# Three numbers of a planner: first products, second keys and token sums of a gated mix of attention and MLP

## The chip, the cores and the metric

The kernel runs on one core of one Trainium2 chip. The metric is the device time of one execution in microseconds (us), the median of several runs. Engines are named as in the profile: PE is TensorE's matmul (PEld its weight load), DVE is VectorE, ACT is ScalarE, POOL is GpSimd, SP is SyncE, whose queue issues the DMAs. L553 is line 553 of the kernel.

## The reference, cut to what matters

The input is x of 2048 tokens by 448. Two branches read it, and a gate per token mixes them. Everything is float32.

```
g = sigmoid((x * gate_w).sum(-1))
# branch A: 16 heads of 28, each token sees 8 keys: itself and 2, 4, ... 14 tokens back
q, k, v = split(x @ wqkv)
logits  = einsum(q, k at those 8 positions) * 28 ** -0.5   # -1e9 before the first token
a = (softmax(logits) weighted sum of v at those positions) @ wo
# branch B: hidden size 1792
h = relu(x @ w1 + b1) ** 2
b = h @ w2 + b2
out = g * a + (1 - g) * b
```

## The kernel before, in words

**Precision.** A float32 matmul is made of three products of float32r parts: high by high, high by low, low by high. So each operand is split: ScalarE writes the high part (a copy), VectorE subtracts it and writes the low part. `split_full` does that from SBUF. `split_copied` (L726) first has ScalarE copy the raw tile into one PSUM bank, the copy bank, and lets VectorE read from there (L738); the bank is single, so the next copy (L733) waits for the low part of the one before.

**Stages.** The 2048 tokens are reordered into four chunks of 512, two of each parity, so that a token's keys all lie in its own parity. Phase A computes q, k and v of chunks 0, 1, 2 and 3 in this order. Chunk 0 is `qkv_first`. Chunks 1 and 3 are two calls of `qkv_two` each, one for two token tiles. Chunk 2 is `qkv_seven`, which forms the 2 by 2 block product with seven products, and for that needs sums of tokens, made by `token_sums(2)` (six steps, 900 apart in the plan: four on VectorE, L962 and L963, then two that split the sums, `s_1` and `s_0`). Each result is evacuated from PSUM by ScalarE (`qkv_evacuate`, L234; `copied`, L428) or added to a stage by VectorE (`added`, L432) and stored to DRAM (`stage_store`, L226) as q_d, k_d, v_d. Within `run`, a VectorE write (`turn`, L211) into an accumulator lets its two row groups change places.

Phase B runs the MLP chunk by chunk, in the order 3, 0, 1, 2: hidden layer (`h_first`, `h_second`), square and split of it (`mlp_ops`, L852 to L855), second layer (`o_part`). Its first two hidden pairs (`mlp_one`, `mlp_two`) are put into the last call of `qkv_two`. Here w1 and w2 are split too (`w1_piece`, `w2_piece`), timed to end before they are read.

**Attention** runs beside all of this. It has eight units: two parities by four groups of four heads. For a unit, `att_load_qk` loads q and k from DRAM (L524, L525) into tiles that have one buffer each. Eight products `qk_piece` on GpSimd (L553) are each reduced by VectorE (L554); a softmax in three steps follows, then eight products with v (`av_piece`, L560), reduced by L568. Products go through a pool of four buffers. `attention` interleaves the units: the qk products of unit i, then the av products of unit i - 1.

**What sets the order.** Nothing is scheduled automatically: each engine runs its instructions in the order in which Python wrote them. Two clocks steer that order. `clock["pe"]` adds the estimated time of each batch of matmuls: `advance(dt)` adds dt, first emits everything that is due (entries of `later`, set by `when` and `at` with planned times in ns), and then lets the attention generator emit as long as `clock["att"]` is behind. Each product yields its planned cost (`QK_COST`, `AV_COST`, `SM_COST`), which moves `clock["att"]`. The costs do not delay anything on the chip; they only decide beside which matmuls, and so behind which other instructions, a product, its reduction or a load is written. `piece` calls `flush(DEFER)` after each product, which emits the oldest reductions until two are left pending.

The generator starts when chunk 1 is stored (`st_["spilled"] = 0`, `clock["on"] = True`). It emits the loads of unit 0 and waits `ATT_DELAY`; then eight products of unit 0 are planned `QK_COST` apart; the loads of unit 1 come directly after the eighth (L659); then it waits `KEY_DELAY` before the first product of unit 1:

```
                if i == 1:
                    yield KEY_DELAY
                q, k = qk.pop(i)
                for s in range(NS):
                    yield piece(lambda: qk_piece(i, q, k, lgs[i], s), QK_COST)
...
                    if i == 0:
                        qk[1] = att_load_qk(*units[1])
```

Other planned times that stand near: `when(82000.0 ...)` of w1's last piece, `when(85500.0, w2_piece, 0, ...)`, the load of the first four rows of w2, and `when(76300.0 ...)` for w1's third piece (L1027 to L1032).

Of the kernel before, what the change touches and what calls it, by code (L numbers as in the profile page):

```python
# [30 lines left out]
MM512 = 227.0  # L31
MM448 = 203.0
QK_COST = 2300.0
AV_COST = 2000.0
SM_COST = 600.0
ATT_DELAY = 17000.0
# [7 lines left out]
LOAD_DELAY = 1500.0  # L44
LAND_DELAY = 5000.0
OL_DELAY = 2500.0
KEY_DELAY = 6000.0
DEFER = 2
ORDER = (3, 0, 1, 2)
WARM = 13  # L50
# [6 lines left out]
def gated_mix_kernel(ctx: ExitStack, tc: tile.TileContext, xT, wqkv, w1, w2, wo, b1, b2, out):  # L57
# [306 lines left out]
    class Group:  # L364
# [12 lines left out]
        def token_sums(self, n, j):  # L377
            a, b = sums[self.c, (None, 1, 0, 0, 1)[n]], (None, 1, 0, 1, 0)[n]
            o = (2 * self.u + b) * P if j < 2 else CH + b * P
            return tuple(t[:, o:o + P] for t in a)  # L380
# [140 lines left out]
    def att_load_qk(par, g):  # L521
        q = attp.tile([P, NS, C], F32, tag="q", name=f"q{par}{g}")
        k = kv_tile("k", f"k{par}{g}")
        nc.sync.dma_start(q, q_d[par, g].rearrange("(p s) c -> p s c", s=NS))  # L524
        nc.sync.dma_start(k, halo_ap(k_d, par, g))  # L525
        return q, k

    def att_load_v(par, g, tag="v"):
        v = kv_tile(tag, f"v{par}{g}")
        nc.sync.dma_start(v, halo_ap(v_d, par, g))  # L530
        return v
# [10 lines left out]
    def flush(n):  # L542

        m = 2
        while len(pending) > n and m:
            if quiet[0] and pending[0] in exps_due:
                return
            pending.pop(0)()
            m -= 1

    def qk_piece(u, q, k, lg, s):
        pr = prodp.tile([P, W, C], F32, tag="pp", name=f"qk{u}_{s}", bufs=PP_BUFS)
        nc.gpsimd.tensor_mul(pr, q[:, s:s + 1].to_broadcast([P, W, C]), k[:, s:s + W])  # L553
        pending.append(lambda: nc.vector.tensor_reduce(  # L554
            lg[:, s], pr.rearrange("p w (h d) -> p w h d", h=HG), axis=AX.X, op=ALU.add))

    def av_piece(u, par, g, v, lg, s):

        pr = prodp.tile([P, C, W], F32, tag="pp", name=f"av{u}_{s}", bufs=PP_BUFS)
        nc.gpsimd.tensor_mul(  # L560
            pr.rearrange("p (h d) w -> p w h d", h=HG),
            lg[:, s][:, :, :, None].to_broadcast([P, W, HG, DH]),
            v[:, s:s + W].rearrange("p w (h d) -> p w h d", h=HG),
        )
        o = o_t[par, s]

        def rest():
            nc.vector.tensor_reduce(o[:, g * C:(g + 1) * C], pr, axis=AX.X, op=ALU.add)  # L568

            def out():  # L570
                nc.vector.transpose(o, o)
                at(OUT_DELAY, lambda: o_store(par, s))
            if g == G - 1 and par:
                out()
            elif g == G - 1:

                at(s * OUT_GAP, out)
        pending.append(rest)
# [5 lines left out]
    def softmax(u, lg):  # L584

        lgv = lg.rearrange("p s w h -> p s h w")
        mx = smp.tile([P, NS, HG], F32, tag="mx", name=f"mx{u}")
        sm = smp.tile([P, NS, HG], F32, tag="sm", name=f"sm{u}")

        def masked():  # L590
            nc.gpsimd.tensor_add(lg, lg, mask[:, :, :, None].to_broadcast([P, NS, W, HG]))
            pending.append(lambda: nc.vector.tensor_reduce(mx, lgv, axis=AX.X, op=ALU.max))

        def exps():
            nc.gpsimd.tensor_sub(lg, lg, mx[:, :, None].to_broadcast([P, NS, W, HG]))

            def rest():
                nc.scalar.activation(lg, lg, AF.Exp, scale=SCALE)

            def sums():  # L600
                nc.vector.tensor_reduce(sm, lgv, axis=AX.X, op=ALU.add)
                nc.vector.reciprocal(sm, sm)
            exps_due.append(rest)
            pending.extend([rest, sums])

        def norm():
            nc.gpsimd.tensor_mul(lg, lg, sm[:, :, None].to_broadcast([P, NS, W, HG]))

        return [masked, exps, norm]
# [9 lines left out]
    def attention():  # L619


        lgs, vs, qk = {}, {}, {}
        n = len(units)
        soft = []

        loads = []

        def piece(fn, cost):
            fn()
            flush(DEFER)  # L630
            while loads and not hold[0]:
                loads.pop(0)()
            return cost

        def soft_step():
            return piece(soft.pop(0), SM_COST)

        for i in range(n + 1):
            if i < n:
                par, g = units[i]  # L640
                while st_["spilled"] < par:
                    yield None
                if i not in qk:
                    qk[i] = att_load_qk(par, g)
                if i == 0:
                    vs[0] = att_load_v(par, g)
                    yield ATT_DELAY
                lgs[i] = smp.tile([P, NS, W, HG], F32, tag="lg", name=f"lg{i}")
                if i == 1:
                    yield KEY_DELAY  # L650
                q, k = qk.pop(i)
                for s in range(NS):
                    yield piece(lambda: qk_piece(i, q, k, lgs[i], s), QK_COST)

                    if soft and (s == 2 or (i == 1 and s in (4, 7))):
                        yield soft_step()
                if i + 1 < n and units[i + 1][0] <= st_["spilled"]:
                    if i == 0:
                        qk[1] = att_load_qk(*units[1])  # L659
                    else:  # L660
                        loads.append(lambda i=i: qk.update({i + 1: att_load_qk(*units[i + 1])}))
                soft.extend(softmax(i, lgs[i]))
            if i >= 1:
                par, g = units[i - 1]
                v, lg = vs.pop(i - 1), lgs.pop(i - 1)
                for s in range(NS):
                    if g == 0:
                        assert len(o_t) < NS
                        o_t[par, s] = opool.tile([P, D], F32, tag="o", name=f"o{par}_{s}", bufs=NS)
                    yield piece(lambda: av_piece(i - 1, par, g, v, lg, s), AV_COST)  # L670
                    if soft and (s in (2, 5) or (i == n - 1 and s == 7)):
                        yield soft_step()
                    if i == n - 1 and s == 1:

                        loads.append(lambda i=i: vs.update({i: att_load_v(*units[i], "k")}))
                if i < n - 1:
                    loads.append(lambda i=i: vs.update({i: att_load_v(*units[i])}))
                if g == G - 1:
                    while pending:
                        flush(0)  # L680
                    st_["att"] = par

    att = attention()
    clock = {"pe": 0.0, "att": 0.0, "on": False}
    later = []
# [227 lines left out]
    def when(t, fn, *args):  # L913
        later.append((t, lambda: fn(*args)))
# [61 lines left out]
    def steps(t, gap, fns):  # L976
        for i, fn in enumerate(fns):
            when(t + i * gap, fn)
# [41 lines left out]
            when(t + 5000.0, lambda c: x_spill(c, xs[c]), c)  # L1020
    when(23500.0, x_more, 2)
    when(39500.0, x_more, 3)
    when(46000.0, lambda: steps(46100.0, 900.0, token_sums(2)))
    when(10500.0, x_spill, 0, x)
    when(25000.0, w1_piece, 0, 38000.0, 2000.0)
    when(44500.0, halos)
# [326 lines left out]
    for g in range(2, 2 * NF):  # L1353
        i, f = g // (NF // 2), g % (NF // 2) * 2
# [121 lines left out]
```

## Time and profile before

| | us |
|---|---|
| median of 3 runs | 417.91 (417.07 to 418.85) |
| the profiled execution's own time | 416.63 |
| its span, first to last instruction | 414.8 |
| TensorE busy | 407.4 |
| GpSimd busy | 267.1 |
| VectorE busy | 279.1 |
| ScalarE busy | 219.8 |

The granted TensorE clock is 1.0 in all slices. The times of rows are microseconds from the span's start. A row of the timeline has the start, the time from the first start to the last end of what it merges, the engine, the line, the operation, output and input with their shapes, and the count; in brackets stands how long the engine was idle before it, and the engine and line that ended the wait. A row of DMA issues ends with the median time from the issue to the landing.

### The profile page before, as it was taken

Reading aid. Unit: us, or ns where it says so; the run is one execution under the profiler, and the core shown is the slowest. Engines: PE = TensorE matmul, PEld = TensorE weight load, DVE = VectorE, ACT = ScalarE, POOL = GpSimd, SP = SyncE. Lnnn points to the kernel's source line nnn. Section 1 sums busy time; section 2 is a strip of 40 time slices with the busy share of each in tenths; the row PEclk is TensorE's granted clock in tenths of the full one; section 3 lists DMA queues with packets and bytes.
Section 4 is the critical chain, followed back from the end, with each engine's and each line's share of the span. In section 5 each row is a group of like instructions: output and inputs, shape, how many; then the busy total and the mean of one; then the engine's idle time right before and its main releaser. Section 6 shows DMA issues by size and latency. Waiting matters only on the chain.

```text
span 414.8 us, 9364 instructions
## 1 busy us (share of the span) xinstructions
PE 407.4 (98%) x3817; PEld 363.9 (88%) x3817; DVE 279.1 (67%) x454; ACT 219.8 (53%) x498; POOL 267.1 (64%) x167
## 2 busy tenths in 40 slices
PE   8999999999799999999999999999999999999997
PEld 8999999989688888888888888989898888888996
DVE  4674874576586867777755897979676677792344
ACT  4674786398475566444565535444643254346640
POOL 0000000960999999989999999899989978950000
PEclk9999999999999999999999999999999999999999
DMA  7999899968263415554020569965146530058304
GB/s 212 344 380 350 237 379 288 373 204 268 92 234 159 158 50 179 204 187 152 2 83 2 175 230 271 259 149 154 36 151 210 205 129 0 31 159 156 103 2 179
DMA packets 66492, 74.00 MB, mean 178 GB/s; under 512 B 32464, under 2 KB 58768, under 8 KB 66320
## 3 DMA queue, kind: packets, MB, share of 16 engines
q1 hardware_dynamic: 66448, 73.39, 55.3%
q8 instruction: 30, 0.49, 0.5%
q14 instruction: 14, 0.11, 0.1%
HBM read 45.94 MB, written 28.25 MB: 179 GB/s over the span
## 4 chain that ended last, share of the span: by engine, by line
PE 89%; DVE 3%; ACT 3%; DMA 2%; POOL 2%; issue 1%; SPq 0%; DVEq 0%; POOLq 0%
PE b L201 32%; PE h L201 30%; PE qkv L201 11%; PE a L201 7%; PE qkv L282 2%; DMA k<-k_d 2%; PE v L335 2%; POOL qk L553 2%; PE x L335 1%; DVE lg L554 1%; PE warm L865 1%; PE a L1248 1%; ACT x L997 1%; PE z L335 1%; DVE st L432 1%
## 5 line engine op out<-in xcount | busy, mean ns | idle before, releaser
L553 POOL TENSOR_TENSOR qk<-q,k 128x896 f32<-128x896 f32 x64 | 134.4, 2129 | 92.3 <-DMA k<-k_d 71.2
L560 POOL TENSOR_TENSOR av<-lg,v 128x896 f32<-128x896 f32 x64 | 118.7, 1954 | 3.3 <-DVE lg L554 2.8
L852 DVE TENSOR_TENSOR h<-h,h 128x512 fp32r<-128x512 f32 x56 | 38.5, 688 | 59.9 <-ACT h L855 59.5
L554 DVE TENSOR_REDUCE lg<-qk 128x32 f32<-128x896 f32 x64 | 67.2, 1075 | 4.8 <-POOL qk L553 4.7
L568 DVE TENSOR_REDUCE o<-av 128x112 f32<-128x896 f32 x64 | 66.7, 1070 | 1.4 <-POOL av L560 1.4
L201 PE MATMUL b<-w2bh,h 64*128 64x448 f32 x448 | 66.2, 360 | 0.4 <-DVE h L852 0.4
L201 PE MATMUL b<-w2ah,h 64*128 64x448 f32 x448 | 66.3, 359 | 0.0
L853 ACT ACTIVATE h<-h,b1z 128x512 f32<-128x512 f32 x56 | 36.7, 656 | 42.1 <-PE h L201 42.1
L201 PE MATMUL qkv<-wqh,x 64*128 64x448 f32 (+1 forms) x384 | 57.7, 361 | 0.6 <-DVE qkv L211 0.6
L201 PEld LDWEIGHTS b<-w2bh,h 64*128 64x128 f32 x448 | 42.0, 184 | 4.3 <-DVE h L852 0.7
L201 PEld LDWEIGHTS b<-w2ah,h 64*128 64x128 f32 x448 | 41.9, 184 | 3.7
L201 PE MATMUL b<-w2bl,h 64*128 64x448 f32 x224 | 40.6, 358 | 0.0
L201 PE MATMUL b<-w2al,h 64*128 64x448 f32 x224 | 40.5, 358 | 0.0
L201 PEld LDWEIGHTS qkv<-wqh,x 64*128 64x128 f32 x384 | 36.6, 184 | 3.7 <-DVE qkv L211 1.1
L201 PE MATMUL qkv<-wql,x 64*128 64x448 f32 (+1 forms) x192 | 35.3, 360 | 0.0
L854 ACT ACTIVATE h<-h 128x512 fp32r<-128x512 f32 x56 | 33.5, 599 | 1.7
L855 ACT ACTIVATE h<-h 128x512 f32<-128x512 f32 x56 | 33.2, 593 | 0.0
L800 ACT ACTIVATE h<-h 128x4 fp32r<-128x4 f32 (+1 forms) x35 | 7.2, 207 | 43.8 <-PE b L201 43.7
L234 ACT ACTIVATE st<-qkv 128x448 f32<-128x448 f32 x36 | 18.2, 542 | 15.8 <-PE qkv L201 9.0
L201 PEld LDWEIGHTS b<-w2bl,h 64*128 64x128 f32 x224 | 21.1, 184 | 1.9
L201 PEld LDWEIGHTS b<-w2al,h 64*128 64x128 f32 x224 | 21.0, 184 | 1.9
L201 PEld LDWEIGHTS qkv<-wql,x 64*128 64x128 f32 x192 | 18.4, 184 | 1.3
(257 smaller groups left out, 829.6 us busy)
## 6 DMA issues: line engine op xcount, KB each, us to landing
k<-k_d SPq DMA_DIRECT2D x8, 840.0 KB, 6.4
v<-v_d SPq DMA_DIRECT2D x8, 840.0 KB, 4.7
x_d<-x SPq DMA_DIRECT2D x12, 512.0 KB, 8.0
q_d<-st SPq DMA_DIRECT2D x8, 448.0 KB, 5.7
k_d<-st SPq DMA_DIRECT2D x8, 448.0 KB, 6.1
v_d<-st SPq DMA_DIRECT2D x8, 448.0 KB, 5.3
w1raw<-w SPq DMA_DIRECT2D x4, 896.0 KB, 9.9
q<-q_d SPq DMA_DIRECT2D x8, 448.0 KB, 3.8
```

The source lines that it names most:

```text
L201: nc.tensor.matmul(acc.pt[:, :acc.n], a[rows], w[rows], start=acc.todo == acc.all, stop=acc.todo == 1)
L234: nc.scalar.activation(st[:, :, t % 2], heads(pt), AF.Copy)
L282: nc.tensor.matmul(acc.pt[:, :D], a, w, start=k == j == 0, stop=False)
L335: nc.tensor.matmul(self.pt[:, :self.n], a, w, start=new, stop=True, skip_group_check=True)
L553: nc.gpsimd.tensor_mul(pr, q[:, s:s + 1].to_broadcast([P, W, C]), k[:, s:s + W])
L554: pending.append(lambda: nc.vector.tensor_reduce(lg[:, s], pr.rearrange("p w (h d) -> p w h d", h=HG), axis=AX.X, op=ALU.add))
L560: nc.gpsimd.tensor_mul(pr.rearrange("p (h d) w -> p w h d", h=HG), lg[:, s][:, :, :, None].to_broadcast([P, W, HG, DH]), v[:, s:s + W].rea ...
L568: nc.vector.tensor_reduce(o[:, g * C:(g + 1) * C], pr, axis=AX.X, op=ALU.add)
L852: nc.vector.tensor_sub(hl, pt, f32(hh))
L853: ops += [lambda pt=pt, r=r: nc.scalar.activation(pt, pt, AF.Relu, bias=b1t[:, f + r:f + r + 1]), lambda pt=pt, hh=hh: nc.scalar.activatio ...
L854: lambda pt=pt, hh=hh: nc.scalar.activation(hh, pt, AF.Square),
L855: lambda pt=pt, r=r, low=low: (nc.scalar.activation(pt, pt, AF.Square), at(delays[r], low))]
```

## The change

Three numbers of the plan change. The products of unit 0 are planned 2130 apart instead of 2300; `KEY_DELAY` grows from 6000 to 7300; and the token sums of chunk 2 are planned from 44,600 on instead of 46,100. No instruction is added or removed, no tile or wait is changed by hand: what changes is the order in which instructions are written into the engines' queues.

```diff
 QK_COST = 2300.0
+QK_FIRST = 2130.0
 AV_COST = 2000.0
...
-KEY_DELAY = 6000.0
+KEY_DELAY = 7300.0
...
                 for s in range(NS):
-                    yield piece(lambda: qk_piece(i, q, k, lgs[i], s), QK_COST)
+                    yield piece(lambda: qk_piece(i, q, k, lgs[i], s), QK_COST if i else QK_FIRST)
...
-    when(46000.0, lambda: steps(46100.0, 900.0, token_sums(2)))
+    when(44500.0, lambda: steps(44600.0, 900.0, token_sums(2)))
```

## The prediction

> **What bounds the kernel now.** I read the page first, then TensorE's waits, then the chain of waits where they fall.
>
> ```profile
> span 414.8 us, 9364 instructions
> ...
> PE 407.4 (98%) x3817; PEld 363.9 (88%) x3817; DVE 279.1 (67%) x454; ACT 219.8 (53%) x498; POOL 267.1 (64%) x167
> ```
> ```profile
> PE h L201 <- ACT st L234: 2.1, 1, 2.1
> ...
> PE qkv L201 <- DVE qkv L211: 0.6, 1, 0.6
> ```
>
> TensorE works 407.4 of 414.8 us. No matmul is added or removed, so the time can change only through the 7.4 us in which it stands still. These two waits are single stalls, of 2.1 and 0.6 (columns: total, times, longest); they are the part that this change can reach. The chain of waits shows what feeds the larger (columns: start, length, what):
>
> ```profile
> 93.90 0.36 SPq L226
> ...
> 94.35 0.46 SPq L226
> ...
> 94.91 0.84 SPq L524
> ...
> 95.80 7.20 DMA k<-k_d
> ...
> 103.16 6.31 POOL qk L553 x3
> ...
> 109.49 1.09 DVE lg L554
> 110.58 0.54 DVE w2al L738
> ...
> 111.14 0.55 ACT copy L733
> 111.69 0.47 ACT st L234
> ...
> 112.20 2.99 PE h L201 x23
> ```
>
> The second unit's keys are asked for at 95.80, behind two stores (93.90, 94.35) that wait for ScalarE. They land at 103.0. GpSimd's third product ends at 109.47; its reduction holds VectorE's queue, behind it stand a low part (L738), ScalarE's copy, and the evacuation (L234) that frees the accumulator for the next hidden layer. TensorE starts at 112.20, and the timeline has the wait to two digits:
>
> ```profile
> 112.20 0.50 PE L201 MATMUL h<-x,w17h 64*128 64x512 f32 x1 [2.14 <-ACT st L234]
> ```
>
> so it had been idle since 110.06. GpSimd, meanwhile, stood still from 89.30 to 103.16:
>
> ```profile
> 72.58 16.72 POOL L553 TENSOR_TENSOR qk<-q,k 128x896 f32<-128x896 f32 x8 [71.19 <-DMA k<-k_d]
> 103.16 6.30 POOL L553 TENSOR_TENSOR qk<-q,k 128x896 f32<-128x896 f32 x3 [13.85 <-DVE w2al L738]
> ```
>
> The second row names a VectorE instruction as releaser. This is it:
>
> ```profile
> 102.40 0.63 DVE L738 TENSOR_TENSOR w2al<-copy,w2ah 128x448 fp32r<-128x448 f32 x1 [0.61 <-ACT copy L733]
> ```
>
> It ends at 103.03, within a few hundredths of the load; a product reads neither of its tiles, so I take the load, as the chain does.
>
> **The change, part by part.**
>
> *The keys' request (QK_FIRST and KEY_DELAY).* The planner's clock stands at 51,156 when attention is switched on, so the first product is planned at 68,155. Eight products of 2300 put the second unit's loads at 86,555; eight of 2130 put them at 85,195. The planning step that covers 85,195 ends at 85,260, the stores are written after the one that ends at 85,869. So both loads now stand ahead of the two stores, and also ahead of the w2 load that was planned for 85,500. They can't run at once: q and k have one buffer each, and the first unit reads them until 72.58 + 16.72 = 89.30. SyncE waits there, then issues q at about 89.3 and k at 89.7. Where they land comes from these rows (size, median us from issue to landing, first of the whole run, then of 86 to 100 us):
>
> ```profile
> k<-k_d SPq DMA_DIRECT2D x8, 840.0 KB, 6.4
> ...
> w1raw<-w SPq DMA_DIRECT2D x4, 896.0 KB, 9.9
> q<-q_d SPq DMA_DIRECT2D x8, 448.0 KB, 3.8
> ```
> ```profile
> w2raw<-w SPq DMA_DIRECT2D x1, 896.0 KB, 5.2
> k<-k_d SPq DMA_DIRECT2D x1, 840.0 KB, 7.2
> ...
> q_d<-st SPq DMA_DIRECT2D x1, 448.0 KB, 2.8
> ```
>
> 448 KB land in 3.8 and 896 KB in 5.2, so 448 KB more cost 1.4. q lands at 93.1, k 2.6 later at 95.7; by k's own medians 96.1 to 96.9. GpSimd starts some 7 us sooner and has three products by 96 + 6.3 = 102.3. The three reductions then follow VectorE's earlier work without waiting: below that work ends 1.04 later than before, at 103.03 + 1.04 = 104.1; three reductions of 1.05 end at 107.2, L738 (0.54), the copy (0.55) and L234 (0.47) at 108.8. TensorE wants the accumulator at 110.06 + 1.04 = 111.1. **The stall of 2.14 goes**, with 2.3 us to spare; k could land as late as 102 before any of it returned. Bounds: -2.14 to 0, I take -2.14.
>
> *What the shorter first products do to VectorE.* Planning unit 0 tighter moves its products to earlier planning steps, and each emission flushes an older reduction into VectorE's queue. The third product moves from the step ending at 73,080 to 72,471, the fourth from 77,343 to 74,907, the fifth (77,355 to 76,675) from 79,779 to 77,343, the eighth from 85,260 to 83,433; the others keep their step. So reduction 0 now precedes the additions of z, reduction 1 those of x, and **reduction 2 moves ahead of the first w1 low part** (L738, planned for 77,600). Before, that queue read:
>
> ```profile
> 78.03 1.15 DVE L432 TENSOR_TENSOR st<-z,st 128x448 f32<-128x448 f32 x2
> 79.09 1.08 DVE L554 TENSOR_REDUCE lg<-qk 128x32 f32<-128x896 f32 x1
> 80.09 1.15 DVE L432 TENSOR_TENSOR st<-x,st 128x448 f32<-128x448 f32 x2
> ...
> 82.14 0.61 DVE L738 TENSOR_TENSOR w1bl<-copy,w1bh 128x448 fp32r<-128x448 f32 x1
> ...
> 88.44 1.08 DVE L554 TENSOR_REDUCE lg<-qk 128x32 f32<-128x896 f32 x1
> ```
> ```profile
> 82.79 0.55 ACT L733 ACTIVATE copy<-w1raw 128x448 f32<-128x448 f32 x1 [0.85 <-DVE w1bl L738]
> ```
> ```profile
> 89.65 0.47 PE L201 MATMUL qkv<-wqh,x 64*128 64x448 f32 x2 [0.57 <-DVE qkv L211]
> ```
>
> GpSimd has product 2 by 72.58 + 3 x 2.09 = 78.9, so nothing waits for it. One reduction (79.09 to 80.09 is 1.00; with its tail 1.08) then stands before the low part, which starts at 83.2 instead of 82.14. ScalarE's copy waited for just that low part; it uses the one copy bank, and copies, low parts and x copies alternate from there without a gap to the fifth reduction at 88.44 and the L211 write behind it, for which TensorE waited 0.57 at 89.08. Reduction 2 used to run later, in a gap that this chain leaves to VectorE while ScalarE works; now it is on the chain. I move the chain by **1.04**: TensorE restarts at 90.7 and the 0.57 becomes 1.6. Bounds: 0 (a gap that I do not see swallows it) and +2.0 (reduction 0 also counts). The swaps of reductions 0 and 1 with additions of the same queue free TensorE's accumulators 1.0 later: z's first at 79.65 for a matmul that began at 79.85. That is a margin of 0.2; without it the cost is under 0.3.
>
> *The w2 load that now stands behind.* It was issued at 93.1 - 5.2 = 87.9 and now comes at 90.2. By the 1.4 per 448 KB it lands 2.8 after k, at 98.5. ScalarE reads it first at:
>
> ```profile
> 96.96 0.60 ACT L732 ACTIVATE w2ah<-w2raw 128x448 fp32r<-128x448 f32 x1
> ...
> 102.64 0.98 ACT L234 ACTIVATE st<-qkv 128x448 f32<-128x448 f32 x2 [0.28 <-PE qkv L201]
> ```
> ```profile
> 103.64 0.40 PE L201 MATMUL h<-x,w17h 64*128 64x512 f32 x2
> ```
>
> that is 98.0 with the shift. It is 0.5 late. Cover: ScalarE idles 0.28 before L234, whose first half (0.49) ends 0.5 before the hidden-layer matmul at 103.64, so 0.75 of lateness is free. I take 0; a load that takes 9.9, like w1raw of the same size, lands at 100.1 and costs 2.1 - 0.75 = 1.35, and 2.25 if both issues ahead take the 0.84 of q's in the chain, so that it starts 0.9 later. The rows show the order this rests on: store, store, q and k, issued at 93.90 to 95.80, land last with k. [...]
>
> *Token sums 1.5 sooner.* Their six ScalarE parts now stand before the evacuation of chunk 1's last q and k:
>
> ```profile
> 54.44 0.98 ACT L234 ACTIVATE st<-qkv 128x448 f32<-128x448 f32 x2 [0.74 <-PE qkv L201]
> 55.45 1.38 ACT L129 ACTIVATE s_1h<-xraw 128x512 fp32r<-128x512 f32 x3
> 56.85 1.38 ACT L129 ACTIVATE s_0h<-xraw 128x512 fp32r<-128x512 f32 x3
> ```
> ```profile
> q_d<-st SPq DMA_DIRECT2D x1, 448.0 KB, 8.9
> ```
>
> They take 2 x 1.38, ScalarE was idle for 0.74 ahead of the evacuation, so this and its stores come some 2.0 later. Attention's first load waits for them, but here the store took 8.9 to land (row of 50 to 60 us) against 2.8 from an idle queue: 6.1 of backlog hides it. I take 0; bounds 0 and, the cover gone, 2.0 on attention's start; sooner sums gain nothing, since TensorE waits for nothing between its start and the 0.57 below 90 us.
>
> *Later products* come 60 ns earlier in the plan (1360 - 1300). By the planner's arithmetic thirteen cross a planning step, and two of their reductions overtake a hidden layer's low part, these:
>
> ```profile
> 132.39 0.69 DVE L852 TENSOR_TENSOR h<-h,h 128x512 fp32r<-128x512 f32 x1 [1.42 <-ACT h L855]
> ```
> ```profile
> 210.56 0.69 DVE L852 TENSOR_TENSOR h<-h,h 128x512 fp32r<-128x512 f32 x1 [1.00 <-ACT h L855]
> ```
>
> VectorE idles 1.42 and 1.00 ahead of them, room for one reduction each: 0, at most 0.1.
>
> **Sum**: -2.14 + 1.04 + 0 + 0 + 0 = -1.1. The profiled execution took 416.63 (414.8 and 1.83 around it), so 415.5 for it; the median of the runs is 417.91, 1.28 above, and I predict 417.91 - 1.1 = **416.8**.
>
> **The rivals.**
> *A. Both effects are gains.* VectorE absorbs reduction 2 and the 0.57 stays or goes: 417.9 - 2.14 to - 2.7 = 415.2 to 415.8. For it: VectorE is two thirds busy. Against: the copy at 82.79 waited for L738.
> *B. The w2 load takes the stall's place.* Landing after 98.75 it makes ScalarE late, and the hidden layer at 104.7 waits. From 99.85 on the change loses: with 1.35, 418.2; with 2.25, 417.9 - 1.1 + 2.25 = 419.1. For it: 1288 KB ahead in the queue. Against: that queue was empty when q is issued.
> *C. Token sums delay attention by 2.0* (the backlog is less than it looks): keys at 97.7 still suffice, but w2raw lands at 100.5, 2.5 late, 1.75 of stall: 417.9 - 2.14 + 1.04 + 1.75 = 418.6. For it: the evacuation does come later. Against: the 6.1.
>
> **How the numbers follow.** Forecast 0.55 (416.2 to 417.4), A 0.2, B 0.17, C 0.08. What a measurement can tell is 0.5%, 2.09 us: faster means under 415.8, slower over 420.0. A lies almost wholly under the first, and a little of the forecast: 0.2. B and C reach the second only if both meet or the load is later still: 0.07. Same 0.73. Range 415.1 (A's faster end and its 0.1) to 418.8 (C, and most of B).
>
> **What would show it.** k's request at about 89.7, ahead of the two stores; GpSimd idle 7 us, not 13.85; no wait for L234 near 110. TensorE's wait for L211 near 89 at 1.6, the decisive row between forecast and A. ScalarE's first L732 on w2 at about 98.5, waiting for its load; a TensorE wait near 104.7 would be B. A first product later than 72.6 would be C. Wrong altogether if the 2.1 is still there with keys in by 97, or if the hidden layers' low parts show new waits after 120.

## The result and the profile after

The kernel after takes 415.47 us (median of 20 executions, 415.0 to 417.99), the kernel before 418.02 (20 executions, 416.74 to 418.85): a ratio of 0.995, 95% interval 0.9937 to 0.9963. That is 2.55 us or 0.6%, with an interval on both sides of the 0.5% that the prediction takes as the least that can be told, and 1.3 below the predicted 416.8. It lies inside the range of 415.1 to 418.8, but below the forecast's own 416.2 to 417.4 and within the 415.2 to 415.8 of rival A, which expected two gains. The profile shows that it is not A. One execution in all that follows, of the kernel with one added product, took 509.54 us at a mean clock of 0.755 and is left out of its counts.

The page of after, its head and its first part:

```profile
span 415.0 us, 9362 instructions
...
PE 407.5 (98%) x3817; PEld 389.4 (94%) x3817; DVE 278.5 (67%) x454; ACT 220.2 (53%) x498; POOL 268.1 (65%) x167
```

The profiled execution took 416.86 us, 0.23 more than the one of before, in spite of the gain. Here are TensorE's waits in it (us in total, times, longest); all lines after 34 stand one higher than before:

```profile
PE qkv L202 <- DVE qkv L212: 1.6, 1, 1.6
...
PE h L202 <- ACT st L235: 0.8, 1, 0.8
PE qkv L283 <- DVE x L896: 0.5, 1, 0.5
```

The wait of 2.1 for L234 (L235 in after) is gone. The 0.6 has become 1.6, as forecast. There is a new 0.8, which is not the old one: it lies near 106, in the hidden layer ahead of it. The 0.5 is the start's, behind the first load of x; no part of the change reaches it, and the profile of before has none.

The timeline of after has the keys' request ahead of everything, and the load of w2 behind it:

```profile
90.19 0.33 SPq L525 DMA_DIRECT2D q<-q_d  x1
90.57 0.42 SPq L526 DMA_DIRECT2D k<-k_d  x1
91.09 0.38 SPq L779 DMA_DIRECT2D w2raw<-w  x1
```
```profile
95.95 6.31 POOL L554 TENSOR_TENSOR qk<-q,k 128x896 f32<-128x896 f32 x3 [5.79 <-DMA k<-k_d]
```

GpSimd idles 5.79 instead of 13.85 and has its third product at 102.26, not 109.47. On VectorE, reduction 2 stands ahead of the first low part (L739, before L738), and TensorE's wait follows:

```profile
82.73 1.07 DVE L555 TENSOR_REDUCE lg<-qk 128x32 f32<-128x896 f32 x1
83.72 0.61 DVE L739 TENSOR_TENSOR w1bl<-copy,w1bh 128x448 fp32r<-128x448 f32 x1
```
```profile
91.22 0.47 PE L202 MATMUL qkv<-wqh,x 64*128 64x448 f32 x2 [1.55 <-DVE qkv L212]
```

The chain of waits of after (start, length, what) shows where the 0.8 comes from:

```profile
91.09 9.73 DMA w2raw<-w
...
105.83 0.53 ACT st L235
...
106.41 2.79 PE h L202 x18
```

The load of w2 took 9.73 us, not the 5.2 of before. It landed at 100.82; ScalarE's first high part of w2 waited for it, and ScalarE with its alternation of high parts and copies was late for the evacuation that TensorE needed:

```profile
100.84 0.58 ACT L733 ACTIVATE w2ah<-w2raw 128x448 fp32r<-128x448 f32 x1 [2.16 <-DMA w2raw<-w]
```
```profile
106.41 0.50 PE L202 MATMUL h<-x,w17h 64*128 64x512 f32 x1 [0.76 <-ACT st L235]
```

That is the mechanism of rival B, in this execution.

**Where the time went, by stage.** TensorE's order is the same in both kernels, so four of its instructions serve as milestones: the last product of y, the first of the hidden layer that starts near 104, the first of the second layer near 118, the last of all. The rows of before (the one at 103.64 stands in the prediction):

```profile
65.64 0.36 PE L335 MATMUL y<-wqh,x 64*128 64x448 f32 x2
...
118.41 0.36 PE L201 MATMUL b<-w2ah,h 64*128 64x448 f32 x2
...
411.40 0.27 PE L1248 MATMUL last<-woh,o 128*128 128x224 f32 x1
```

and of after:

```profile
66.23 0.36 PE L336 MATMUL y<-wqh,x 64*128 64x448 f32 x2
...
105.26 0.39 PE L202 MATMUL h<-x,w17h 64*128 64x512 f32 x1
...
118.32 0.36 PE L202 MATMUL b<-w2ah,h 64*128 64x448 f32 x1
...
411.63 0.27 PE L1249 MATMUL last<-woh,o 128*128 128x224 f32 x1
```

From y to the hidden layer: 38.00 us before, 39.03 after, +1.03. From there to the second layer: 14.77 before, 13.06 after, -1.71. The rest: 292.99 and 293.31. So the two forecast effects are both there. Yet 14.77 - 13.06 holds a gain and the late load in one number, and neither it nor the forecast -1.1 explains 2.55 between the medians. The experiments take these apart.

### The profile page after: what moved, and what is told of

It is laid out like the page before. It is cut to its first block, busy times and chain, and to the rows that moved or that the text cites. A ratio compares the mean times of both kernels' runs of the same rounds, so it can differ in the third digit from the quotient of the medians.

```text
span 415.0 us, 9362 instructions
## 1 busy us (share of the span) xinstructions
PE 407.5 (98%) x3817; PEld 389.4 (94%) x3817; DVE 278.5 (67%) x454; ACT 220.2 (53%) x498; POOL 268.1 (65%) x167
## 4 chain that ended last, share of the span: by engine, by line
PE 89%; DVE 3%; DMA 3%; ACT 2%; issue 1%; SPq 0%; DVEq 0%
PE b L202 32%; PE h L202 32%; PE qkv L202 11%; PE a L202 7%; DMA w2raw<-w 2%; PE qkv L283 2%; PE v L336 2%; PE x L336 1%; DVE lg L555 1%; ACT copy L734 1%; DMA xraw<-xT 1%; PE a L1249 1%; PE z L336 1%; DVE st L433 1%; PE y L336 1%
## 5 line engine op out<-in xcount | busy, mean ns | idle before, releaser
L202 PE MATMUL b<-w2ah,h 64*128 64x448 f32 x448 | 74.3, 359 | 0.0
L202 PE MATMUL b<-w2bh,h 64*128 64x448 f32 x448 | 72.9, 360 | 0.4 <-DVE h L853 0.4
L202 PEld LDWEIGHTS b<-w2ah,h 64*128 64x128 f32 x448 | 57.5, 184 | 0.4
L202 PEld LDWEIGHTS b<-w2bh,h 64*128 64x128 f32 x448 | 54.5, 184 | 1.7 <-DVE h L853 0.7
L202 PE MATMUL b<-w2al,h 64*128 64x448 f32 x224 | 53.8, 358 | 0.0
L202 PE MATMUL b<-w2bl,h 64*128 64x448 f32 x224 | 51.4, 359 | 0.0
L202 PEld LDWEIGHTS b<-w2al,h 64*128 64x128 f32 x224 | 33.1, 184 | 0.1
L202 PEld LDWEIGHTS b<-w2bl,h 64*128 64x128 f32 x224 | 31.0, 184 | 0.4
L235 ACT ACTIVATE st<-qkv 128x448 f32<-128x448 f32 x36 | 17.9, 542 | 15.2 <-PE qkv L202 12.3
```

The source lines that it names most:

```text
L202: nc.tensor.matmul(acc.pt[:, :acc.n], a[rows], w[rows], start=acc.todo == acc.all, stop=acc.todo == 1)
L235: nc.scalar.activation(st[:, :, t % 2], heads(pt), AF.Copy)
```

## The experiments

The same milestones were read for each profile, in the same way; the table gathers the start of the last product of y and the three differences, in us. "Clock" is the mean granted TensorE clock of that execution.

| kernel | y at | y to hidden layer | hidden layer to second layer | rest | clock |
|---|---|---|---|---|---|
| before | 65.64 | 38.00 | 14.77 | 292.99 | 1.0 |
| before, again | 67.99 | 37.98 | 16.09 | 293.19 | 0.996 |
| after | 66.23 | 39.03 | 13.06 | 293.31 | 1.0 |
| after, again | 65.37 | 38.99 | 12.05 | 292.98 | 1.0 |
| keys alone | 67.97 | 37.98 | 13.37 | 293.26 | 1.0 |
| products alone | 66.04 | 39.04 | 14.79 | 293.04 | 1.0 |
| token sums alone | 65.94 | 37.98 | 16.14 | 293.33 | 0.996 |
| after, w2 first | 65.73 | 39.17 | 12.05 | 293.01 | 0.999 |
| keys alone, w2 first | 65.96 | 38.02 | 12.05 | 293.01 | 1.0 |
| before, seven added products | 65.64 | 37.96 | 14.82 | 293.15 | 1.0 |

The first column differs by up to 2.6 us between executions, with the change and without it, and the 1.74 between after and the keys alone arise in the first 15 us: in the keys alone products still start 0.37 us apart beyond 8 us, in after 0.20 apart from about 6.4 us on, with a mean granted clock of 1.0 in both executions. Two products in a row show it by their length, 0.95 and 0.56:

```profile
8.12 0.95 PE L282 MATMUL qkv<-wql,x 128*128 128x448 f32 x2
```
```profile
7.15 0.56 PE L283 MATMUL qkv<-wql,x 128*128 128x448 f32 x2
```

Why they start farther apart is not settled. So the profiled executions' own times (417.74 for the keys alone, with a median of 415.62) can't be compared; the stages and the medians can.

### The change in parts

**The whole change again.** No edit.

> The changed kernel once more, beside its parts. Theory 1 (the forecast's steps): -1.1 to -2.2 us against the kernel before; TensorE's waits are about 1.55 at L212 near 91 us, none for L235 near 110, and 0 to 0.8 for L235 near 106, as late as the w2 load lands. Theory 2 (the reduction moved ahead costs nothing, everything comes from the keys): the wait at L212 is back at 0.6 in an execution whose first matmul does not wait. Theory 3 (the size is set by how fast loads land in an execution): the span and the wait near 106 move together with the landing time of the w2 load, between 5 and 10 us.

415.63 us, ratio 0.9941 [0.9918, 0.9964]. TensorE's wait for L212 was 1.6 again, which rules out theory 2. In this profile the load of w2 was issued at 89.86 and took 7.5 us by the view of DMA issues, and ScalarE, busy until its first high part of w2, did not wait for it:

```profile
w2raw<-w SPq DMA_DIRECT2D x1, 896.0 KB, 7.5
```
```profile
97.64 0.60 ACT L733 ACTIVATE w2ah<-w2raw 128x448 fp32r<-128x448 f32 x1
```

TensorE had no wait near 106, and the stage took 12.05. So the late load costs 1.0 (13.06 - 12.05) in one execution and nothing in another of the same kernel.

**The keys alone.** The eighth product's planned cost is lowered instead of all eight, so that the loads come early and no reduction moves; the token sums stay.

```diff
-                    yield piece(lambda: qk_piece(i, q, k, lgs[i], s), QK_COST)
+                    yield piece(lambda: qk_piece(i, q, k, lgs[i], s), QK_COST if i or s < NS - 1 else QK_COST - 1360.0)
...
-KEY_DELAY = 6000.0
+KEY_DELAY = 7300.0
```

> Only the request of the second unit's keys moves ahead of the stores and the w2 load; the eighth product's planned cost is cut by 1360 instead of 170 per product, so that VectorE's order around the first unit stays that of before; token sums as before. Theory 1: wait near 89 stays 0.57, wait near 110 goes (-2.14), but ScalarE is 1.0 earlier at the w2 rows than in the changed kernel, so a w2 load that lands at 98.5 to 100.8 costs 0.8 to 3.1 near 104; in all -1.3 to +1, and not better than the changed kernel by more than 0.5. Theory 2: -2.1, the same as the changed kernel.

415.62 us, ratio 0.9949 [0.9927, 0.9972]: as good as the whole. That is 2.6 below the median of before beside it (418.23), more than theory 1's -1.3 to +1 allows; below is why. From y to the hidden layer it has before's 37.98, so the price of the shorter products is not paid. But its w2 load, behind the keys as in after, was late in the profile:

```profile
101.84 0.58 ACT L732 ACTIVATE w2ah<-w2raw 128x448 fp32r<-128x448 f32 x1 [2.46 <-DMA w2raw<-w]
```

and the next stage took 13.37 instead of 12.05. ScalarE, without the 1.04 of delay, reaches this load sooner, which fits the larger price (1.32 here, 1.01 in after): what the keys alone save at one place they pay in part at the other.

**The shorter products alone.** The first seven products are planned 2130 apart, the eighth makes up the difference, so that the loads stay where they were.

```diff
-                    yield piece(lambda: qk_piece(i, q, k, lgs[i], s), QK_COST)
+                    yield piece(lambda: qk_piece(i, q, k, lgs[i], s), QK_COST if i else 2130.0 if s < NS - 1 else 3490.0)
...
-KEY_DELAY = 6000.0
+KEY_DELAY = 5940.0
```

> Only the products of the first unit are planned 2130 apart; the loads of the second unit keep their place in SyncE's queue (the eighth product's planned cost takes up the rest), token sums as before. Theory 1: the wait at L211 near 89 grows from 0.57 to 1.55, the wait near 110 stays but is filled from the other side: the evacuation is 1.0 later as well, so the whole is +0.5 to +1.1. Theory 2: 0, the wait near 89 stays at 0.6.

419.57 us, ratio 1.0035 [1.0012, 1.0058]: slower, by an interval that leaves out no change, and 1.3 above the median of before beside it, a little more than the expected +0.5 to +1.1. Its timeline has the forecast wait, 1.53 against 0.57 before, and the old stall unchanged behind it:

```profile
91.03 0.47 PE L201 MATMUL qkv<-wqh,x 64*128 64x448 f32 x2 [1.53 <-DVE qkv L211]
```
```profile
113.68 0.50 PE L201 MATMUL h<-x,w17h 64*128 64x512 f32 x1 [2.17 <-ACT st L234]
```

**The token sums alone.**

```diff
-    when(46000.0, lambda: steps(46100.0, 900.0, token_sums(2)))
+    when(44500.0, lambda: steps(44600.0, 900.0, token_sums(2)))
```

> Only the token sums are planned 1500 sooner. Theory 1: 0 (-0.3 to +0.3): the evacuation of chunk 1's last q and k ends 2.0 later, the stores wait in a full queue anyway, and attention's first product starts at 72 to 73 us as before. Rival (the sums matter): a first product later or sooner by over 0.5 us, or a change of over 0.5 us in the time.

418.41 us, ratio 1.0004 [0.9982, 1.0026]: nothing. GpSimd's first product starts at 72.65, as expected. Its profile has waits of 2.2 and 0.6, as before; and yet its stage from the hidden layer to the second layer took 16.14 us, 1.37 more than in the profile of before. The end of its stall and the windows of that stretch (window, its length, busy time and count of PE, PEld, DVE, ACT, POOL, then the granted clock of TensorE, the DMA share and GB/s) show why:

```profile
112.55 0.50 PE L201 MATMUL h<-x,w17h 64*128 64x512 f32 x1 [2.21 <-ACT st L234]
```
```profile
110.00:112.00 2.00, 0.34 (x3) 0.00 (x0) 1.45 (x2) 0.51 (x2) 2.00 (x2) 1.00 0.00 0
112.00:114.00 2.00, 1.45 (x12) 1.22 (x14) 1.29 (x3) 2.00 (x6) 2.00 (x2) 0.99 0.28 95
114.00:116.00 2.00, 2.00 (x12) 1.53 (x12) 2.00 (x3) 1.97 (x4) 2.00 (x3) 0.50 1.02 332
116.00:118.00 2.00, 2.00 (x16) 1.86 (x14) 1.96 (x4) 1.52 (x5) 2.00 (x2) 0.65 0.10 33
118.00:120.00 2.00, 2.00 (x20) 1.73 (x19) 1.69 (x2) 1.20 (x5) 2.00 (x2) 1.00 0.00 0
```

Some 1.4 us behind the end of the stall (112.55; by the 0.99 the fall lies near 113.96), TensorE's granted clock falls to a half, and then is full again. Work lost: 2 x (0.01 + 0.50 + 0.35) = 1.72 us, which at half clock is 3.4 us of time. In before's profile it was 1.00 in all of these windows. From its first hidden-layer product to its last of all this kernel took 309.47, before 307.76: 1.71 more. TensorE's busy time shows it too, 409.2 against 407.4 with the same number of instructions, while the time in which it stood still hardly differs (7.6 and 7.4):

```profile
PE 409.2 (98%) x3817; PEld 397.2 (95%) x3817; DVE 279.2 (67%) x454; ACT 220.1 (53%) x498; POOL 267.6 (64%) x167
```

### The clock behind the stall

This gave a second theory of the gain: the stall near 110 has a price beyond its length, because in some executions the clock drops behind it. The results give the mean clock of every execution timed for the experiments; here those at 0.995 or 0.996 are called low and the others full. Over 116 executions of before, 56 had 0.995 or 0.996, with a median of 418.75 us, and 60 had 0.999 or 1.0, with 416.98: 1.77 apart, the 1.72 of the windows. Kernels without the stall (after, after again, the keys alone: 44 executions) were at 0.998 or above in every one; with the stall kept, 9 of 12 (products alone) and 7 of 12 (token sums alone) were low. Full with full and low with low, the products alone are 1.2 and 1.1 us above the executions of before beside them, close to the forecast price of 1.04 (3 and 9 executions); the token sums alone are 0.2 and 0.1 above. Six runs test it.

**Before, again.** No edit.

> The kernel before against itself: ratio 0.998 to 1.002. Theory 'clock': about half of its executions have a mean granted clock of 0.995 to 0.996 and take some 1.7 us longer than those at 0.999 to 1.0; where the profiled execution is one of them, the clock is at about half speed from some 1.5 us behind the end of the idle stretch near 110 for about 3.3 us, and nowhere else. Theory 'waits only': the two groups have the same time, or the low clock lies elsewhere.

417.79 us, ratio 0.9995 [0.9971, 1.0018]. 5 of 12 executions were low (median 418.84) and 7 full (416.81). The profiled one was low, and its windows have the same picture in the same place, behind a stall of 2.14; to its last product it took 309.28 from the first of the hidden layer, 1.52 more than in before's profile:

```profile
114.54 0.50 PE L201 MATMUL h<-x,w17h 64*128 64x512 f32 x1 [2.14 <-ACT st L234]
```
```profile
114.00:116.00 2.00, 1.46 (x12) 1.19 (x14) 1.30 (x3) 2.00 (x6) 2.00 (x2) 0.92 0.29 96
116.00:118.00 2.00, 2.00 (x12) 1.56 (x10) 2.00 (x3) 1.97 (x4) 2.00 (x3) 0.50 1.02 332
118.00:120.00 2.00, 2.00 (x18) 1.80 (x16) 1.95 (x4) 1.31 (x5) 2.00 (x2) 0.73 0.10 31
```

**Work put into the stall.** Seven products ahead of the block that stalls, into the bank that is free; the wait for the other bank ends when it did.

```diff
-    def h_first(x, c, f):
+    def h_first(x, c, f, fill=0):
...
         accs = [Acc("m", f"h{c}_{f + r}", CH) for r in range(2)]
+        for _ in range(fill):
+            nc.tensor.matmul(accs[0].pt[:, :CH], w17h[0:64, f // 2 * P:f // 2 * P + P], x.x7[0:64], start=True, stop=True)
...
-        pair[1] = h_first(xm[3], ORDER[0], 2)
+        pair[1] = h_first(xm[3], ORDER[0], 2, fill=7)
```

> The kernel before with seven more products of 64 x 512 put on TensorE just before the first real product of the block that stalls near 110 (same operands as that product, into its own bank, which the real product then starts anew); every other engine has the same instructions in the same order. Each takes about 0.23 us by the rows near 109, so they fill 1.6 us of the 2.14 us for which TensorE stands idle near 110, and the product that waits for the bank freed at 112 starts when it did. Theory 'clock' (the idle stretch near 110 halves TensorE's granted clock for about 3.3 us behind it in about half of the executions, as in the profile of the token sums alone, where 1.7 us were lost between 114 and 118): the mean granted clock is 0.998 to 1.0 in every execution instead of 0.995 to 0.996 in about half of them, and the median falls by 0.7 to 1.7 us, ratio 0.996 to 0.9985. Theory 'waits only' (the split of the granted clock has to do with the execution, not with the stall): no change, ratio 0.999 to 1.001, and half of the executions at 0.995 to 0.996. Both: the wait for the bank near 112 ends when it did.

416.92 us, ratio 0.9968 [0.9948, 0.9987], and 0 of 12 executions low. The waits of TensorE fall to

```profile
PE h L201 <- ACT st L234: 0.6, 1, 0.6
```

while the stage takes 14.82, as in before: no time was saved at full clock (416.92 against 417.08 for the full-clock executions of before beside it), and the median still fell by 1.5. Before beside it had 14 of 23 low. It is the clock that was saved. This kernel does only useless work more, and is faster.

**Less work in the stall.** One such product, then three, and three again on another chip.

> The kernel before with one more product of 64 x 512 ahead of the block that stalls near 110 (seven left 0.6 us of the 2.1 us of waiting and no execution with a lowered clock). It leaves about 1.9 us. Theory 'clock by length': the share of executions with a lowered granted clock falls from about half to something between none and half, and each such execution still loses about 1.8 us; the median lies between 416.9 and 418.7 accordingly. Rival 'a threshold between 1.6 and 2.1 us that this passes': the share stays at about half, or is none.

> The same with three more products, which leave about 1.45 us. The kernel after waits 1.55 us near 91 and no execution of it had a lowered clock, so by either theory none is expected here: all executions at 0.998 to 1.0 and a median of 416.8 to 417.1. If some are lowered, the length of the wait alone does not decide it.

> The three half products again, on the same chip as the whole ones. Both theories: 4 to 6 of 12 executions with a lowered clock, those about 1.8 us longer than the others. None, or all, would say that the share differs too much from chip to chip to be compared.

Ratios 0.9993 [0.9971, 1.0015], 1.0001 [0.9979, 1.0023] and 1.0003 [0.998, 1.0025]. Low executions: 3 of 11, 5 of 12 and 4 of 12 (before beside them 9 of 23 and 9 of 23). With so few executions, 3 of 11 can't be told from 9 of 23. The expectation for three products was wrong: the profiled waits were 1.2 (a full execution) and 1.6 us (a low one), like the 1.55 of after near 91 or shorter, and none of after's executions was low. So the length of the wait alone does not decide it.

**Three products over the whole array.** The same three, over 128 rows of the array instead of 64.

```diff
-            nc.tensor.matmul(accs[0].pt[:, :CH], w17h[0:64, f // 2 * P:f // 2 * P + P], x.x7[0:64], start=True, stop=True)
+            nc.tensor.matmul(accs[0].pt[:, :CH], w17h[:, f // 2 * P:f // 2 * P + P], x.x7, start=True, stop=True)
```

> The three added products ahead of the block near 110, now over all 128 rows of the array instead of 64 (same time each, bank and place). With three of 64 rows the wait was 1.2 us and 5 of 12 executions had a lowered clock, although the kernel after waits 1.55 us near 91 and had none in 32. Theory 'work in the window': what lowers the clock is how little the array did over some microseconds, and products over half of its rows count half; counted so, the kernel before loses 2.5 us of work there, three half products leave 2.2, seven (no lowered execution) 1.7, and three whole ones 1.8: no or few lowered executions, at most 2 of 12, median 416.8 to 417.2. Theory 'time in the window': whole products count as half ones, 4 to 6 of 12 lowered, median 416.8 to 418.5. In both the wait is 1.2 us and the time of the executions at full clock 416.3 to 417.5.

417.34 us, ratio 0.9996 [0.9976, 1.0017]; 0 of 12 low, against 9 of 24 with the half products. But the wait was not the expected 1.2. The waits of the whole products and, below, of the half ones on the same chip:

```profile
PE h L201 <- ACT st L234: 0.9, 1, 0.9
```
```profile
PE h L201 <- ACT st L234: 1.6, 1, 1.6
```

So this fits the theory that work is what counts, but work and length of the wait were both changed, and it does not separate them. The median shows no gain here: its executions, all full, were 0.3 above the full ones of before (417.34 against 417.02), and at 417.32 the median of before lay just on the full side of its two groups (14 full, 9 low).

### The late load, and a better kernel

**After, with w2 first.** The load is due 0.5 us sooner in the plan, and so is written ahead of the second unit's q and k.

```diff
-    when(85500.0, w2_piece, 0, 4, 92500.0, 1400.0)
+    when(85000.0, w2_piece, 0, 4, 92500.0, 1400.0)
```

> The kernel after with the w2 load due 0.5 us sooner in the plan, so that SyncE issues it ahead of the second unit's queries and keys instead of behind them. The load then lands about 2 us or more sooner and its first high part no longer waits for it; the keys are asked for 0.6 us later and land about 0.6 to 1 us later, GpSimd's first product of the second unit with them, still ahead of the VectorE work that the products feed. Theory 'w2 load late': the wait near 106 (0.76 us in one profile of after, none in the other) is gone in every execution, median 0 to 0.8 us below after's, that is 414.8 to 415.6, ratio 0.992 to 0.994. Rival 'keys late again': a part of the wait near 110 comes back, 415.6 to 417.

415.11 us over 6 executions, ratio 0.993 [0.9904, 0.9957]. w2 landed in 5.4 us and k in 7.6 (view of DMA issues), GpSimd started at 97.81, and no stall came back: the only single waits are 1.5, the known 1.2 at the start and 0.4. The stage takes 12.05.

**The keys alone, with w2 first.** The edit of the keys alone and this one together.

> The kernel before with the second unit's keys asked for early by the cost of the eighth product alone (no reduction moves ahead on VectorE, token sums where they were) and with the w2 load due 0.5 us sooner, so that SyncE issues it ahead of these queries and keys. By theory it has the gain of the change (no wait near 110, clock at full speed) without its two prices: the wait near 89 stays at 0.6 us instead of 1.6, and the w2 load does not make the products near 104 wait (1.1 us in the profile of the early keys alone). Expected: 0.5 to 1.1 us below the keys alone, 414.5 to 415.1, ratio 0.990 to 0.9925. Rival 'the waits are taken up by a later one': 415.4 to 415.9, as after.

414.14 us (6 executions, 413.9 to 414.56), ratio 0.9907 [0.9878, 0.9936]: better than expected, and below both kernels. The waits and the milestones of its profile:

```profile
PE warm L865 <- DVE b1z L863: 1.2, 1, 1.2
PE qkv L201 <- DVE qkv L211: 0.6, 1, 0.6
PE b L201 <- DVE h L852: 0.4, 1, 0.4
```
```profile
65.96 0.36 PE L335 MATMUL y<-wqh,x 64*128 64x448 f32 x2
...
103.98 0.40 PE L201 MATMUL h<-x,w17h 64*128 64x512 f32 x2
...
116.03 0.36 PE L201 MATMUL b<-w2ah,h 64*128 64x448 f32 x2
...
409.04 0.27 PE L1248 MATMUL last<-woh,o 128*128 128x224 f32 x1
```

38.02 and 12.05: the gain without the two prices. Against the full-clock executions of before beside it (417.08) it is 2.94, and by stage 14.77 - 12.05 = 2.72.

## Why the prediction was right or wrong

The two stated effects are there, each with its sign and in its place. The time, however, missed the forecast's 416.2 to 417.4 and fell among rival A's times, although A's mechanism did not occur; that it is inside the range is partly luck, since the range reached so low only for A's sake.

**The keys' request: right in mechanism, too small.** Requests (90.19 and 90.57 for 89.3 and 89.7), GpSimd's 5.8 of idle time for "7, not 13.85" and the vanished stall came as forecast. The term was -2.14 and measured -2.72. What failed is that I took the length of the wait for its price. The rows of before around the stall were in reach:

```profile
109.68 0.39 PE L201 MATMUL h<-x,w17h 64*128 64x512 f32 x1
112.20 0.50 PE L201 MATMUL h<-x,w17h 64*128 64x512 f32 x1 [2.14 <-ACT st L234]
112.21 0.73 PE L201 MATMUL h<-x,w17l 64*128 64x512 f32 x2
112.55 0.62 PE L201 MATMUL h<-x,w17h 64*128 64x512 f32 x2
```

Of the pair of products that should start together, the one of the other bank went ahead alone at 109.68, and the wait is counted from its end in the profile (109.68 + 0.39 = 110.07). The partner started at 112.20, 112.20 - 109.68 = 2.52 late; in the keys alone with w2 first, without the stall, the two start together:

```profile
110.03 0.39 PE L201 MATMUL h<-x,w17h 64*128 64x512 f32 x2
```

The remaining 0.20 is not settled; the first rows behind the stall are also wider apart than usual (112.21 to 112.55, 0.34, where steps near it take 0.23), which would be half of it.

**What the shorter first products do to VectorE: right.** +1.04 forecast; +1.03 in after, +1.04 in the products alone, with the wait at 1.55 and 1.53. This is the part of the change that makes the kernel slower, and it fells rival A, whose times hold the measured one.

**The w2 load: taken as nothing, and it was not.** Its order in the queue was right; its landing was forecast at 98.5, with 0.75 of cover, and "a load that takes 9.9" as the bad case. It took 9.7, 9.2 and 7.5 us from its issue in three profiles with the keys ahead and 5.3 to 5.4 in two with it first. The step that failed is "2.8 after k": it landed some 5.0, 4.4 and 2.7 us after k. Why the first two are so late is open; two stores were issued at 95.48 and 95.94 in after, while w2 was under way, and no run tests their part. Its price was 1.01 and 1.32 in two of the three (13.06 and 13.37 against 12.05) and none in the third. So rival B happens, in part of the executions, and does not take the whole gain. The median of after with the load first was 0.4 to 0.5 lower (415.11 against 415.47 and 415.63), but by 6 executions, and not measured beside after.

That a load pays for what is put ahead of it was the prediction's estimate, and the runs agree with the direction: w2 took 5.3 to 5.4 us with its load first, 7.5 to 9.7 behind the keys.

**Token sums: right**, nothing; rival C did not occur. Its sign, a first product later than 72.6, did show in the profile of after (73.42), but most of that is this execution's late start, with y 0.59 later than in before; in after again it was 72.22. **Later products: right**, within the profiles' reach: the rest is 292.98 in after again and 292.99 in before, with the full clock in both.

**What the sum lacked.** At full clock the terms are -2.72 + 1.03 and 0 to 1.0 for the load, that is -0.7 to -1.7; measured against the full-clock median of before (416.98), after's 415.47 is -1.5. The forecast of -1.1 lies in this. The rest, from 416.98 to the 418.02 of before, is the clock: the stall made nearly half of the executions 1.8 us longer, and the change ends that. The prediction's first step, that "the time can change only through the 7.4 us in which it stands still", left this out: TensorE's busy time itself grows when the clock falls, to 409.2 in the token sums alone. It then set its working on one profile with a full clock, saw its execution 1.28 below the median of the runs, and carried this difference over unchanged. That was the wrong step: most of the difference, 417.91 - 416.98 = 0.93, was itself an effect of the stall. The clocks of the runs of before behind this first median are not on record, so this rests on the 116 others.

## What to carry to other kernels

Price a stall by TensorE's progress between two milestones, start to start, not by its entry among the waits: 2.14 there was 2.72 here, and some 1.5 to 1.7 more where the clock dropped. If a profiled execution is faster than the median of the runs, ask what else those runs do before carrying the difference over: here each run's mean clock told two groups apart. And where loads change places in a queue, look for the cheapest order of all of them: the 896 KB ahead of the 1288 KB delayed the keys (k took 7.6 and 7.2 us to land, 5.2 to 5.3 with the keys first), but by nothing that TensorE waited for.

## What the hardware showed that was not expected

Behind a stall of 2.1 to 2.2 us TensorE's granted clock fell to 0.50 for some 3.4 us (the 1.72 and 1.70 us of work lost by the two sets of windows, at half clock), beginning 1.1 to 1.4 us after work had resumed, in the two profiles shown; by their mean clock of 0.995 or 0.996, 56 of 116 executions of the kernel before had it, and none of the 56 executions of kernels without this stall (0.998 or above). What decides whether an execution is hit, these runs do not show. Seven products over half of the array's rows in the stall, or three over all, left 0 of 12 executions low; three over half left 9 of 24. That half-row products count as less work would fit these counts, but the whole ones also left a shorter wait (0.9 against 1.2 and 1.6), so it is not shown.
